# Seven half products instead of a plain second product in 14 of 18 expert slots, with the first expert's slots beside attention and the second's behind it

## The chip, the cores and the metric

The kernel runs on one core of a Trainium2 chip. The metric is the device time of one execution in microseconds. The engines are named as in the profile: PE (TensorE, the matrix engine; PEld is its loading of weights), DVE (VectorE), ACT (ScalarE), POOL (GpSimd) and SP (SyncE, which here only issues DMAs). Each engine works through its own instructions in the order in which the kernel issues them, and semaphores tie the engines together.

## The reference

Windowed attention, followed by a mixture of experts in which every row goes to one expert. All data are float32.

```python
# q, k, v: (8, 8, 576, 64): batch, heads, positions, head width
scores = q @ k.T / 8            # a position sees itself and the 63 before it
attn   = softmax(scores) @ v
x      = attn, rows of 8 heads side by side      # (4608, 512)
logits = x @ w_gate + modality_bias[modality_id] # 8 experts
e      = argmax(logits);  gate = softmax(logits)[e]
out[i] = gate[i] * (relu(x[i] @ w1[e]) @ w2[e])  # w1: 512 x 1024, w2: 1024 x 512
```

The two modalities have biases that favour one expert each, so most rows go to two experts. The kernel calls the one with the larger lead X (or 0) and the other Y (or 1), and picks them on the chip from the biases.

## The kernel before, in words

**Attention.** The 4608 rows are 36 pairs of 64-row blocks, one pair (128 rows) per step `s` of the main loop; two steps are a group `G` (256 rows). Step `s` does the scores of pair `s`, the transposed probabilities of pair `s-1`, the values of `s-2`, the logits of `s-3`; steps 36 to 39 only finish. In odd steps the group `R = (s-5)/2` is routed: `route2` (matmuls on PE that count ranks), `route3` (small DVE operations, queued in the list `routing`, the last of which write the rows' target index and scatter them by POOL's indirect DMA into `xs`, a DRAM buffer ordered by expert). `tick(n)` issues n of these small operations; five or six at a time.

**Slots.** Expert work is done in slots of 256 rows (two tiles `t` of 128). A slot loads its rows from `xs` into the one buffer `xt`, transposes them (`x_part`), takes the first product in four quarters `first(sl, k, i)`, k = 0 to 3, each two pieces i (12 matmuls of 256 columns, in three terms of high and low parts, since every operand is split into two numbers of the type fp32r), a relu on ACT and a low part on DVE, and then the second product. In a plain slot the second product is eight pieces `second(sl, k, t)` of 6 matmuls of 512 columns. In a slot marked `fast` it is seven products of halves (a Winograd form of Strassen's scheme): `left_of` and `right_of` make parts and sums of the four blocks of the hidden rows, `rest_of` two more, `product` takes p1 to p7, each 12 matmuls of 256 columns, and `fast_out` adds them into the output tiles with the gate. The sums of the four blocks of W2 that this needs are made in `combine`.

**Order.** The generator `slot_pieces` yields after each piece, 16 to a plain slot and 15 to a fast one. From step `FIRST = 12` on the main loop calls it at four fixed gaps of a step (`gap`), between attention's parts, and behind attention the last `while` loop runs it to its end. Work of other engines that follows a piece is put into `later` and issued at the next `run_later`. The order on every engine is this issue order. PSUM has eight banks: two for "tp", one each for "sp0", "sp1", "av", "em", "y0" and "y1". `bank(i)` gives the first product's bank: "em" for even quarters, and for odd ones "em" as well while the list `last` is empty, which is so during attention, then "sp0".

**Which slot holds what.** `EARLY` names the groups T after whose scatter a count is taken and a slot is planned (`plan`), and for which of X and Y. The load of such a slot waits only for the scatters up to T (`scatter_after_T`). `LATE` lists slots behind attention: two of X; then the two Y slots that were held back; three of any expert, and a half slot. So there are X, X, X, X, Y, Y, Y, Y, X, X, X, X, X, Y, Y, any, any, any, half; the fast ones are the five X slots from the ninth on (`MIXED = 7`). Rows that these leave would go to a loop with a dynamic trip count at the end (lines 1445 to 1532); it makes no trip here, and the profile has no instruction of it.

**Weights.** Both experts' weights lie in SBUF as high and low parts (`Whi`, `Wlo`), loaded in 32 pieces (`weights`, `split_hi`, `split_lo`) from step 4 on. Behind attention the "any" slots' pieces are swapped in place (`swaps`). The eight `pads` copy rows of padding behind each expert's rows in `xs`; no late slot is loaded before them.

## Time and profile before

| what | value |
|---|---|
| time, three runs | 645.15 us median (641.67 to 645.71) |
| profiled execution, its own time | 640.05 us |
| its span, first to last instruction | 638.3 us |
| PE busy | 611.4 us, 96% |
| DVE busy | 403.5 us, 63% |
| ACT busy | 328.5 us, 51% |
| POOL busy | 154.3 us, 24% |
| matmuls | 6689 |
| granted PE clock | 0.999 of full |

Attention's last scores are at about 332 us, its last logits at some 358 us, and what follows to 638 us is expert slots alone. A row of groups has the line, the engine, the operation, the tiles out<-in, shapes and count, then busy microseconds, mean nanoseconds of one, and the idle time before them with what ended it. A row of a timeline has its start, its length, engine, line, operation and tiles, and in brackets the engine's idle time before it and what ended it. The chain of waits follows the work that ended last back to what released it. Matmuls are pipelined: their listed durations overlap, and distances between starts give the pace.

### The profile page before, as it was taken

To read this page: it belongs to the slowest core of one execution; us is meant where nothing else is said; L and a number is where in the kernel's file an instruction comes from. 1 tells how busy PE (TensorE), PEld (TensorE's weight loads), DVE (VectorE), ACT (ScalarE), POOL (GpSimd) and SP (SyncE) were. 2 spreads that over 40 slices of the span, in tenths; PEclk is the share of its full clock that TensorE was granted. 3 is DMA by queue.
4 is the path that set the end of the run, shared out by engine and by line. 5 is a ranking of instruction groups with operands and counts; after the bars stand their busy time and mean duration, and the time that the engine had idled before them with its cause. 6 is when DMAs were issued, how large, how long until landed. Compare 5 with 4: busy or idle time off the path is not lost. (4 is left out here: it accounts for less than half of the span.)

```text
span 638.3 us, 17909 instructions
## 1 busy us (share of the span) xinstructions
PE 611.4 (96%) x6689; PEld 558.0 (87%) x6689; DVE 403.5 (63%) x1571; ACT 328.5 (51%) x1005; POOL 154.3 (24%) x337
## 2 busy tenths in 40 slices
PE   6898888999999999999999999999999999999996
PEld 3787777898989889899898988999999989989886
DVE  2978977666776676756654255876746755666611
ACT  3888876656665656455644123533433444554411
POOL 5324432042032213320322255111011011101102
PEclk9999999999999999999999999999999999999999
DMA  9989894774876674552323476021105076777300
GB/s 170 184 194 249 233 222 133 180 167 121 184 177 151 140 177 106 142 137 57 111 75 110 123 205 242 20 67 51 50 34 198 16 223 198 211 243 240 109 1 36
DMA packets 142120, 90.72 MB, mean 142 GB/s; under 512 B 118954, under 2 KB 118992, under 8 KB 141904
## 3 DMA queue, kind: packets, MB, share of 16 engines
q1 hardware_dynamic: 133344, 70.07, 44.8%
q0 software_dynamic: 5856, 18.92, 8.0%
q10 hardware_dynamic: 2832, 0.59, 0.6%
q8 instruction: 53, 0.87, 0.6%
q14 instruction: 35, 0.29, 0.2%
HBM read 70.11 MB, written 23.91 MB: 147 GB/s over the span
## 5 line engine op out<-in xcount | busy, mean ns | idle before, releaser
L290 PE MATMUL em<-xh,Whi 128*128 128x256 f32 x400 | 102.8, 291 | 1.2 <-DVE xl L196 1.0
L290 PE MATMUL em<-xh,Wlo 128*128 128x256 f32 x400 | 98.2, 279 | 0.0
L765 ACT ACTIVATE ss<-ss,mn 128x128 f32<-128x128 f32 x240 | 94.0, 397 | 2.6 <-DVE mn L753 2.6
L429 POOL DMA_INDIRECT out_dram<-y,id x36 | 37.5, 1042 | 219.3 <-DVE y L394 74.4
L415 PE MATMUL y<-Whi,hh 128*128 128x512 f32 x208 | 86.6, 416 | 0.0
L415 PE MATMUL y<-Wlo,hh 128*128 128x512 f32 x208 | 81.6, 392 | 2.2 <-DVE e_take L154 2.2
L415 PE MATMUL y<-Whi,hl 128*128 128x512 f32 x208 | 81.5, 392 | 0.0
L290 PEld LDWEIGHTS em<-xh,Whi 128*128 128x128 f32 x400 | 75.3, 188 | 2.2 <-DVE xl L196 1.6
L290 PEld LDWEIGHTS em<-xh,Wlo 128*128 128x128 f32 x400 | 75.4, 188 | 0.5
L774 ACT COPY pT<-tp 128x512 f32<-128x512 f32 x59 | 32.6, 589 | 78.6 <-PE tp L595 74.3
L753 DVE CUSTOM_DVE_ANT_0 ss<-sp,masks 128x128 f32<-128x128 f32 x240 | 53.5, 287 | 18.4 <-PE sp L736 16.2
L301 DVE SCALAR_TENSOR_TENSOR hl<-em,hh 128x512 fp32r<-128x512 f32 x40 | 27.6, 690 | 57.1 <-ACT hh L300 57.1
L290 PE MATMUL em<-xl,Whi 128*128 128x256 f32 x400 | 63.2, 280 | 0.0
L892 POOL DMA_INDIRECT xs_scratch<-xa,idx x36 | 36.2, 1007 | 81.4 <-DVE lm L835 26.2
L290 PEld LDWEIGHTS em<-xl,Whi 128*128 128x128 f32 x400 | 53.7, 188 | 0.0
L791 PEld LDWEIGHTS av<-ve,pT 128*64 128x64 f32 x576 | 36.3, 138 | 16.4 <-issue 8.4
L300 ACT ACTIVATE hh<-em 128x512 fp32r<-128x512 f32 x40 | 23.6, 591 | 48.1 <-PE em L290 44.1
L791 PE MATMUL av<-ve,pT 128*64 128x64 f32 x576 | 41.0, 225 | 7.2 <-DVE ve L666 3.3
L415 PEld LDWEIGHTS y<-Whi,hl 128*128 128x128 f32 x208 | 39.0, 188 | 8.8
L765 ACT ACTIVATION_READ_ACCUMULATOR ss<-ss,mn 128x1 f32 x240 | 46.4, 193 | 0.0
L415 PEld LDWEIGHTS y<-Wlo,hh 128*128 128x128 f32 x208 | 39.2, 189 | 7.6 <-DVE e_take L154 2.5
L415 PEld LDWEIGHTS y<-Whi,hh 128*128 128x128 f32 x208 | 39.1, 188 | 5.6 <-ACT Whi L112 0.3
(341 smaller groups left out, 1535.3 us busy)
## 6 DMA issues: line engine op xcount, KB each, us to landing
xt<-xs_scratch SPq DMA_DIRECT2D x18, 514.0 KB
y<-in_moe_w_dram SPq DMA_DIRECT2D x32, 256.0 KB
vo<-in_v_dram SPq DMA_DIRECT2D x27, 256.0 KB
vo<-in_moe_w_dram SPq DMA_DIRECT2D x27, 256.0 KB
ss<-in_moe_w_dram SPq DMA_DIRECT2D x27, 256.0 KB
pT<-in_moe_w_dram SPq DMA_DIRECT2D x18, 256.0 KB
xs_scratch<-xs_scratch SPq DMA_DIRECT2D x8, 514.0 KB
qk<-in_q_dram SPq DMA_DIRECT2D x16, 256.0 KB
```

What stands on the lines that cost most here:

```text
L290: nc.tensor.matmul(out=hb[:, i * TP:(i + 1) * TP], lhsT=w[buf][:, c0:c0 + P], rhs=x[:, c * TP:(c + 1) * TP], start=(n == 0), stop=(n == le ...
L300: nc.scalar.activation(out=hh, in_=hb, func=AF.Relu),
L301: nc.vector.scalar_tensor_tensor(out=hl, in0=hb, scalar=0.0, in1=hh.bitcast(F32), op0=ALU.max, op1=ALU.subtract)))
L415: nc.tensor.matmul(out=sl["y", t], lhsT=h[:, i * TP + t * P:i * TP + (t + 1) * P], rhs=w[buf][:, c0:c0 + DM], start=(k == 0 and n == 0), s ...
L429: ins = nc.gpsimd.indirect_dma_start(out=out, out_offset=bass.IndirectOffsetOnAxis(ap=sl["id"][:, t:t + 1], axis=0), in_=y, in_offset=None ...
L753: nc.vector.tensor_tensor_reduce(out=ss[a][:, hp, :], in0=sp[a][:, hp * P:(hp + 1) * P], in1=mask, scale=-1.0 / 8.0, scalar=3.0e38, op0=AL ...
L765: nc.scalar.activation(out=ss[a][:, hp, :], in_=ss[a][:, hp, :], func=AF.Exp, bias=mn[:, h:h + 1], scale=-1.0, accum_out=sm[:, h:h + 1])
L774: nc.scalar.copy(out=pT, in_=pp)
L791: nc.tensor.matmul(out=av[c * W64:(c + 1) * W64, 2 * hp + a], lhsT=pT[:, i:i + W64], rhs=(vo if c else ve)[p][:, 2 * hp + a, :], start=Tru ...
L892: ins = nc.gpsimd.indirect_dma_start(out=xs, out_offset=bass.IndirectOffsetOnAxis(ap=idx[:, j:j + 1], axis=0), in_=xg[j], in_offset=None)
```

## The change

All slots beside attention are now X's, at T = 2, 4, ..., 16, and one more X slot follows; then seven slots of Y, two of any expert and the half slot: again 18 full slots and a half. Slots 0 and 1 are plain; the 14 from the third X slot to the last Y slot are fast, five of them wholly beside attention. A piece order of its own is used there (`late7` is false): quarter 1 and quarter 2 follow one another, p7 stands ahead of quarter 3, and the first product's relu for the next slot is queued behind p3. The parts of `right_of` that make sums are a function of their own, `sums_of`, queued later by `after`. Products have only "y0" and "y1" while attention runs.

Only X's weights are loaded beside attention. Their memory is cut into other tiles: `M0` to `M3` hold X, `S0` X's sums of W2, `S1` and `S2` the parts of the fast slots beside attention. X's sums are made in steps 16 to 19, Y's in steps 36 to 39 (`SUMS`). Y's weights come behind attention: the first matrix during slot 7, into `S1` and `S2`; the second during slot 8, over X's first matrix. The padding is ten copies instead of eight: X's and Y's first, which the late X and the Y slots wait for; the others during slots 10 to 12.

```diff
-    EARLY = ((2, (0, 1)), (4, (0, 1)), (6, (0, 1)), (8, (0, 1)), (9, (1, 2)), (10, (1, 2)), (11, (1, 2)),
-             (12, (0, 2)), (13, (0, 2)), (15, (0, 2)))
+    EARLY = tuple((T, (0, 1)) for T in (2, 4, 6, 8, 10, 12, 14, 16))
...
-    LATE = ((0, False), (0, False), (0, True), (1, True), (0, True), (1, True))
-    NPIN = 2
+    LATE = ((0, False),) + ((1, False),) * 7 + ((2, True), (3, True), (2, True))
+    NPIN = 7
...
+    PLAIN = 2
...
-    stock = [wpool.tile([P, 2 * WC], F32, name=f"W{part}1") for part in ("hi", "lo")]
-    Whi = [wpool.tile([P, 2 * WC], F32R, name="Whi0"), None]
-    Wlo = [wpool.tile([P, 2 * WC], F32R, name="Wlo0"), None]
+    stock = [wpool.tile([P, 2 * WC], F32, name="S0")] + [wpool.tile([P, WC], F32, name=f"S{n}") for n in (1, 2)]
+    w_x = [wpool.tile([P, WC], F32R, name=f"M{n}") for n in range(4)]
+    store = {0: w_x}
...
+    def run_after():
+        later.extend(after)
+        after.clear()
...
-        fast = n_slots[0] > MIXED and buf == 0 and whichever is None
+            fast=n_slots[0] > PLAIN and whichever is None, n=n_slots[0] - 1)
...
             if i == 1 and sl["fast"]:
                 later.append(lambda: (left_of if k < 2 else right_of)(sl, k % 2, hb))
+                if k >= 2:
+                    after.append(lambda: sums_of(sl, k % 2, hb))
...
+        def sums_of(sl, k, hb):
+
+            if "s1" not in sl:
+                sl["s1"] = [att.tile([P, ROW], F32R, name=f"xa{i}")[:, 0:512] for i in (0, 4)]
             a12, a22 = halves_of(hb)
             a11, a21 = halves_of(sl["r", k])
             nc.vector.scalar_tensor_tensor(out=a21, in0=a22, scalar=0.0, in1=a21, op0=ALU.max, op1=ALU.add)
             nc.vector.tensor_tensor(out=a11, in0=a21, in1=a11, op=ALU.subtract)
+            s4 = sl["t"][:, k * TP:(k + 1) * TP].rearrange("p (c t) -> p c t", t=P)
+            nc.vector.scalar_tensor_tensor(out=s4, in0=a12, scalar=0.0, in1=a11, op0=ALU.max, op1=ALU.subtract)
             parts(a21, sl["s1"], k)
...
+            order = ("p1", "p7", "p2", "p4", "p5", "p6", "p3")
+            i = order.index(nm)
+            if last:
+                home, n = ("y0", "y1", "sp1", "av")[i % 4], i // 4
+            else:
+                home, n = ("y0", "y0", "y1", "y1")[i % 4], i % 2
...
             if sl["fast"]:
+                for k in (1, 2):
+                    for i in range(2):
+                        first(sl, k, i)
+                        yield
+                fast_step(sl, "p1")
+                run_after()
                 yield
+                late7 = bool(last)
+                if not late7:
+                    fast_step(sl, "p7")
+                    yield
+                first(sl, 3, 0)
                 yield
                 nxt = fetch()
                 first(sl, 3, 1)
                 yield
+                if late7:
+                    fast_step(sl, "p7")
+                    run_after()
+                    yield
                 fast_step(sl, "p2")
+                run_after()
+                if late7:
+                    later.append(lambda: rest_of(sl, "s2"))
                 yield
                 fast_step(sl, "p4")
+                later.append(lambda: rest_of(sl, "s4" if late7 else "s2"))
                 yield
                 x_part(nxt, 0)
                 run_later()
                 x_part(nxt, 1)
+                if last:
+                    run_later()
                 fast_step(sl, "p5")
+                if not late7:
+                    later.append(lambda: rest_of(sl, "s4"))
                 yield
                 fast_step(sl, "p6")
                 yield
                 first(nxt, 0, 0)
                 yield
                 first(nxt, 0, 1)
+                if not late7:
+                    after.append(later.pop())
                 yield
                 fast_step(sl, "p3")
+                run_after()
                 yield
...
-            pieces.extend((x, c) for x in range(2) for c in PIECE_ORDER)
+            pieces.extend((0, c) for c in PIECE_ORDER)
...
+    SUMS = {FIRST + 4 + j: (0, j) for j in range(4)}
+    SUMS.update({NPR + j: (1, j) for j in range(4)})
...
-        n_tick = 6 if s < FIRST else 5
+        n_tick = 6 if s < FIRST or j else 5
...
+    last.append(True)
+    tick(ready_p - issued[0], table=True)
+    pad_rows(pads.pop(0))
...
+    at_ = begin_of[slot_y - 2] + 1
+    for c in (0, 2, 4, 6, 1, 3, 5, 7):
+        task(at_, whole_piece(1, c, 1), load(at_, c, lambda: evs[1]))
+    at_ = begin_of[slot_y - 1] + 7
+    pairs_y = [[load(at_, 8 + j + 4 * i, lambda: evs[1]) for i in range(2)] for j in range(4)]
+    for n in range(6):
+        if n < 4:
+            task(at_, y_quarters(n), *pairs_y[n])
+        if 0 < n < 5:
+            task(at_, lambda x, y: combine(x, y, False), *pairs_y[n - 1])
+        if n > 1:
+            task(at_, y_fourth(n - 2), *pairs_y[n - 2])
```

The weights of the "any" slots follow in the same way as tasks, one piece of work to a step of the `while` loop: the first one's spread over slots 10 to 14 into `M2`, `M3` and `S0`, the others' during the plain slots 16 and 17.

## The prediction

> **What bounds the kernel now.** I read the page first, for which engine is full and when.

> ```profile
> span 638.3 us, 17909 instructions
> PE 611.4 (96%) x6689; PEld 558.0 (87%) x6689; DVE 403.5 (63%) x1571; ACT 328.5 (51%) x1005; POOL 154.3 (24%) x337
> PE   6898888999999999999999999999999999999996
> DVE  2978977666776676756654255876746755666611
> PEclk9999999999999999999999999999999999999999
> ```

> PE is full from the eighth slice (about 112 us) to the last but one, at full granted clock; the loads before that and the end are not touched by the change. So the time is the sum of PE's work plus every wait that is put into PE's queue. Next I read the chain of waits in order of time, which after attention is PE alone, and gives each slot's length (rows: start, length, what).

> ```profile
> 461.06 2.81 PE em L290 x24
> ...
> 476.56 1.44 PE sp L374 x12
> ...
> 482.99 2.81 PE em L290 x24
> ...
> 527.96 2.81 PE em L290 x24
> 530.78 1.38 PE y L415 x6
> ...
> 550.96 2.81 PE em L290 x24
> ```

> From one first product's second quarter to the next slot's, a slot by seven products takes 482.99 - 461.06 = 21.93 us, a plain one 550.96 - 527.96 = 23.00 us: 1.07 us apart. The third view is the busy time of stretches: attention without any weights work, seven-product slots, and plain slots with weight pieces. The last row is the DVE time of line 119 alone, the weight pieces, in the third stretch.

> ```profile
> 240.00:280.00 40.00, 40.00 (x530) 35.99 (x532) 25.20 (x122) 21.71 (x80) 11.24 (x22) 1.00 0.49 121
> 440.00:480.00 40.00, 40.00 (x346) 40.00 (x345) 23.15 (x53) 15.97 (x35) 4.91 (x12) 1.00 0.11 41
> 520.00:560.00 40.00, 40.00 (x268) 36.31 (x267) 25.40 (x42) 19.73 (x37) 5.86 (x12) 1.00 0.67 210
> ...
> 520.00:560.00 40.00, 16.33 (x27) 1.00 0.67 210
> ```

> The columns after the stretch are PE, PEld, DVE, ACT, POOL. DVE needs 23.15 x 21.93/40 = 12.7 us for a seven-product slot and (25.40 - 16.33) x 23.00/40 = 5.2 us for a plain one: 7.5 us more. In attention a slot lasts some 41 us (four steps), and DVE there has 40 - 25.2 = 14.8 us free in 40. So DVE would go to about 32.5 of 40: it is not the bound by its sum, but it and ACT answer PE more slowly, and the question is who waits for an answer.

> **The change, part by part.**

> *The arithmetic.* 14 slots instead of 5 lose one piece each: 9 x 1.07 = 9.6 us off PE, wherever they lie, as PE is full throughout. The trace's rows under it are 1.44 us for 12 matmuls of 256 columns and 1.38 us for 6 of 512, 120 and 230 ns each. [...]

> *Where the slots lie.* From step 13 on a step runs four pieces, so piece p after the first four is in step 13 + (p-1) div 4, at gap (p-1) mod 4. Slots 0 and 1 stay plain (pieces 1 to 32), slots 2 to 5 are by seven products in full attention (33 to 92), slot 6 in steps 36 to 39 (93 to 107), slots 7 to 15 behind attention. Those behind attention behave as the five of before, whose 21.93 us hold no stall. Inside attention two things differ, both unknown to this trace and priced from its nearest rows.

> *One PSUM bank for the first product.* While `last` is empty `bank(0)` and `bank(1)` are both "em", with one buffer. A plain slot puts two second-product pieces between two quarters of the first product. The new order issues quarter 2 straight behind quarter 1 (waiting for the relu of `left_of`), and quarter 1 of the next slot behind p3, with that relu queued only after p3; and p2 straight behind quarter 3 needs that quarter's relu and its low part. The rows show when these answers come today. Each case is a piece of PE, and ACT's relu and DVE's low part for the quarter before it:

> ```profile
> 231.34 0.47 PE L415 MATMUL y<-Whi,hh 128*128 128x512 f32 x1
> 231.81 0.59 ACT L300 ACTIVATE hh<-em 128x512 fp32r<-128x512 f32 x1
> 232.43 0.69 DVE L301 SCALAR_TENSOR_TENSOR hl<-em,hh 128x512 fp32r<-128x512 f32 x1 [0.30 <-ACT hh L300]
> ...
> 265.41 0.48 PE L415 MATMUL y<-Whi,hh 128*128 128x512 f32 x1
> 266.40 0.58 ACT L300 ACTIVATE hh<-em 128x512 fp32r<-128x512 f32 x1
> 267.02 0.69 DVE L301 SCALAR_TENSOR_TENSOR hl<-em,hh 128x512 fp32r<-128x512 f32 x1 [1.58 <-ACT hh L300]
> ...
> 295.49 0.58 ACT L300 ACTIVATE hh<-em 128x512 fp32r<-128x512 f32 x1
> 295.54 0.48 PE L415 MATMUL y<-Whi,hh 128*128 128x512 f32 x1
> ...
> 296.24 0.68 DVE L301 SCALAR_TENSOR_TENSOR hl<-em,hh 128x512 fp32r<-128x512 f32 x1
> ...
> 354.56 0.48 PE L415 MATMUL y<-Whi,hh 128*128 128x512 f32 x1
> ...
> 354.67 0.60 ACT L300 ACTIVATE hh<-em 128x512 fp32r<-128x512 f32 x1 [0.76 <-PE em L290]
> ```

> The relu ends behind the start of the next piece by 1.06 us after gap 0 (ACT does xaT's copy first), 1.57 after gap 2 (exps and a copy first), 0.53 after gap 1, and 0.71 near the end of attention; after gap 3 the long stretch of attention covers it. Today that costs nothing, since the next piece is in another bank. With the change these are PE waits. By the gaps above, quarter 2 behind quarter 1: slot 2 at gap 1 (0.53), slot 3 at gap 0 (1.06), slot 5 at gap 2 (1.57), slot 4 covered. Quarter 1 behind p3: after slot 2 at gap 2 (1.57), slot 3 at gap 1 (0.53), slot 4 at gap 0 (1.06), slot 5 covered. Together 6.3 us. p2 needs the low part at its ninth matmul, 8 x 0.12 = 0.96 us in: slot 3 at gap 2, 267.71 - 265.41 - 0.96 = 1.34; slot 4 at gap 1, 296.92 - 295.54 - 0.96 = 0.42; slot 5 at gap 0, 233.12 - 231.34 - 0.96 = 0.82; 2.6 us. Slot 6 adds two of 0.71, 1.4 us. The bounds of these eleven: nothing if ACT came earlier; and, with more in ACT's and DVE's queues,

> ```profile
> L308 ACT CAST ve<-xa 128x256 fp32r<-128x256 f32 x20 | 8.1, 406 | 3.8 <-DVE xa L348 2.8 <-DVE masks L154 0.7
> ```

> two more such parts (0.41 us each) ahead at each of the nine places in full attention, 7.3 us more. I take four of these eighteen, 1.6 us, as a seven-product slot spreads its parts over four steps and few can stand right ahead of a relu.

> *Rows of group 16 for slot 7.* EARLY now ends at T = 16, whose rows are scattered in step 37; slot 7's load is fetched at piece 100 (gap 3 of step 37), and its transposes are piece 103 (gap 2 of step 38). Only two steps of little attention lie there. The rows show the chain of such a load, and the routing matmul of step 37:

> ```profile
> 106.57 0.17 DVE L904 CAST idx<-dst 128x2 int32<-128x2 f32 x1
> 109.08 0.97 POOL L892 DMA_INDIRECT xs_scratch<-xa,idx  x1 [0.28 <-POOL xa L891]
> 112.57 0.39 SPq L206 DMA_DIRECT2D xt<-xs_scratch  x1
> 116.41 0.19 POOL L274 COPY gate<-xt 128x2 f32<-128x2 f32 x1 [3.89 <-DMA xt<-xs_scratch]
> ...
> 354.51 0.19 PE L863 MATMUL tp<-oh,ones 128*128 128x16 bf16 x2
> 355.97 0.15 DVE L873 TENSOR_TENSOR tgt<-tp,ebase 128x16 f32<-128x16 f32 x1
> 356.46 0.22 DVE L886 RECIPROCAL xa<-se 128x1 f32<-128x1 f32 x2
> 357.47 0.64 PE L816 MATMUL tp<-wg,xaT 128*64 128x8 f32 x16
> ...
> L394 DVE SCALAR_TENSOR_TENSOR y<-y,gate,y 128x512 f32<-128x512 f32 x10 | 7.5, 747 | 0.4
> ```

> From the index to rows in SBUF: 116.41 - 106.57 = 9.8 us. From routing matmul to index: 0.7 us of small operations (355.97 to 356.68) behind one 0.75 us output of p7 (line 394), and the index itself, now within the step, as its ticks go from 5 to 6: 1.7 us. PE has in that time the quarter 3 pair (2.8), the logits of step 38 (0.6), p2 and p4 (2.9): 6.3 us. So PE waits 9.8 + 1.7 - 6.3 = 5.2 us. Bounds: 3 us if nothing lies ahead of the index and the load is quicker, 8 if POOL's new subtractions stand before the scatter. Slot 6 (T = 14) has a step of full attention more, and none is counted. SP waits behind this scatter with the Y sums of step 39 queued behind the load; they go to slot 9 and are early by far.

> *Work with cover.* Y's 16 pieces leave attention, and X's sums enter in steps 16 to 19, on engines that are not the bound: nothing. Y's pieces go to slots 7 and 8: 12.7 + 8 x 16.33/27 = 17.5 us of DVE in 21.9: covered; without cover it would be the 4.8 us. The X pad, its wait on SP and slot 8's load have ten pieces, 14 us, after attention: nothing taken, 4 us as the upper bound. The ten pads instead of eight, and table operations moved to slots 9 to 13: DVE has over 4 us free in each slot. The last slots (two plain, a half) are as before.

> *The sum.* -9.6 + 6.3 + 2.6 + 1.4 + 1.6 + 5.2 = +7.5 us. The profiled execution took 640.05 us (span 638.3 and 1.8 around it), under the median of the runs shown, 645.15 (641.67 to 645.71). It becomes 647.6, and on the median's level 652.7.

> What speaks most against this change beside the waits themselves is what a wait may bring. The longest that the waits view has for PE is

> ```profile
> PE y L415 <- DVE e_take L154: 2.2, 1, 2.2
> ```

> and the granted clock is 9 in every slice. [...]

> **The rivals.**

> *Forecast*: waits outweigh the gain, 652.7; its own range 648 to 660. Chance 0.50.

> *The waits stay covered* (not slower): ACT gets the relu early enough, because the exps move away from it once PE is held, and only the load costs: 645.15 - 9.6 + 5.2 = 640.8; with the load early as well, 635.5. For: DVE has 14.8 us in 40 free in attention, ACT 18.3. Against: each relu in the rows above ends after the next piece began. It decides where the relu ends before PE reaches the next em piece. Chance 0.12, two thirds of it at 635.5.

> *Waits as large as the gain*: the lower row (0.53) at the nine places in attention, 4.8, with 1.4 and a load wait of 3: -0.4, 645. Chance 0.20.

> *DVE becomes the bound in attention.* Its queue is in order, and it stands idle at a head that waits for ACT:

> ```profile
> DVE hl L301 <- ACT hh L300: 82.4, 45, 4.9
> ```

> 1.8 us each time. A seven-product slot has some eight heads of that kind where a plain one has four. Four more at 1.8 put 32.5 of 40 to 39.7, and any burst then is PE's: 2.5 us more a slot in slots 2 to 5, 10 us, 663. Against: waits shrink when a queue is behind. Chance 0.12.

> *Half clock behind the 5.2 us wait*: as long a stretch at half rate adds 2.6 us, 655.6. No row bears it out. Chance 0.04. *A group's count does not fill its slot*, a slot runs on dummy rows, and another is paid for at 23.0 us: 676. All early slots of before were full, as the fallback loop left no row. Chance 0.02.

> **How the numbers follow.** The predicted time is the forecast's, 652.7. The range 640 to 664 takes in the covered case down to its load wait, and the DVE case; it leaves out 0.08 below and some 0.07 above. About 1% (6.5 us) is what a measurement tells from no change. Faster: the fully covered case, 0.08. Same: its rest 0.04, the equal case 0.20, and the forecast's part below 651.6, 0.14: 0.38. Slower: 0.54.

> **What would show it.** Right: in steps 21 to 34 PE matmuls of line 290 idle on ACT's relu, a fraction to 1.6 us each, and p2 on DVE's low part; one PE wait of 4 to 6 us for the load of xt near the end of attention; slots behind it at 21.9 us. Wrong: PE's idle in attention no larger than before, transposes of slot 7 not waiting, or DVE above 37 of 40 in attention.

## The result: 714 us instead of 644, and the profile after

The changed kernel took **714.37 us** (711.16 to 715.27), the kernel before **644.06 us** (641.67 to 645.71) beside it: a ratio of 1.109, interval 1.103 to 1.114. The forecast was 652.7, with a range from 640 to 664. The direction was right and the size was far off: +70 us where +7.5 was worked out.

The page of the changed kernel, where the profiled execution took 715.27 us (span 713.5 and 1.8 around it):

```profile
span 713.5 us, 18839 instructions
PE 640.4 (90%) x7010; PEld 596.4 (84%) x7011; DVE 474.9 (67%) x1755; ACT 363.0 (51%) x1109; POOL 177.3 (25%) x365
PE   6898799999988898998879868798699999999996
DVE  2879867767657576685567553868867777657662
PEclk9999999999998999999999979799899999999999
```

PE was full from the eighth slice on; now it has holes from slice 12 (196 us) to slice 29 (517 us), and only behind them is it full again. The clock strip shows that something else is gone: two slices at 7 and two at 8.

The waits of PE, longest sums first (who waits, for what: us, times, longest):

```profile
PE y L398 <- DVE y L418: 8.5, 6, 2.7
PE y L398 <- ACT y L416: 6.5, 4, 1.9
PE em L292 <- ACT S L340: 6.3, 7, 1.2
PE y L398 <- ACT xa L312: 5.7, 1, 5.7
PE sp L398 <- ACT hh L352: 5.2, 2, 2.7
PE em L267 <- DMA xt<-xs_scratch: 4.8, 3, 4.2
...
PE em L292 <- DVE xl L196: 3.1, 2, 2.0
...
PE sp L398 <- DVE hl L353: 2.1, 2, 1.8
```

Line 292 is the first product, 398 the seven products, 267 the transposition of a slot's rows. The third and the sixth row are terms of the forecast: 6.3 us where 6.3 was forecast, and 4.8, of which one wait of 4.2, where 5.2 was. The first two, 15.0 us, are not in it at all, nor are the fourth, the fifth and the one for `xl`, 14.0 us, of which 13 lie behind attention (1.0 us of the one for `xl` stands ahead of slot 1, as before the change).

Two stretches in full attention (PE, PEld, DVE, ACT, POOL, then the granted clock, DMA share and GB/s) answer to the row at 240 us of the prediction:

```profile
200.00:240.00 40.00, 34.22 (x363) 31.91 (x362) 24.94 (x111) 21.04 (x74) 6.09 (x14) 0.87 0.32 81
240.00:280.00 40.00, 35.02 (x455) 32.65 (x455) 26.54 (x115) 22.12 (x76) 5.49 (x14) 0.96 0.37 93
```

PE lacks 5 to 6 us in 40, and the clock is at 0.87 and 0.96. DVE is busy for 25 to 27 of 40 us, hardly more than before: nobody is full, everybody waits.

The length of each slot, worked out from the timeline as the time from the first transposition of one slot's rows to that of the next (us):

| slot | before | after | after again (693) | e1 tiles | e3 tail | e7 all four | e8 plain, tail | e18 |
|---|---|---|---|---|---|---|---|---|
| 2 | 43.2 | 48.9 | 44.3 | 41.8 | 44.3 | 41.8 | 42.9 | 42.9 |
| 3 | 43.9 | 52.3 | 50.4 | 47.5 | 50.4 | 44.8 | 42.9 | 42.9 |
| 4 | 43.1 | 51.6 | 47.8 | 45.2 | 47.8 | 49.4 | 42.9 | 42.9 |
| 5 | 40.9 | 51.7 | 48.7 | 43.4 | 48.7 | 41.2 | 40.6 | 40.6 |
| 6 | 29.9 | 43.3 | 41.5 | 40.1 | 41.6 | 42.0 | 29.9 | 29.9 |
| 7 | 23.1 | 38.8 | 39.1 | 36.5 | 33.5 | 26.3 | 25.2 | 23.8 |
| 8 | 21.9 | 22.6 | 24.0 | 22.0 | 22.4 | 22.3 | 22.0 | 23.9 |
| 9 | 22.3 | 26.3 | 24.9 | 24.8 | 27.3 | 27.3 | 27.2 | 22.7 |
| 10 | 21.9 | 29.4 | 29.3 | 29.3 | 21.9 | 22.0 | 21.9 | 23.5 |
| 11 to 15, each | 21.9 to 23.1 | 21.9 | 21.9 | 21.9 | 21.9 | 21.9 | 21.9 | 21.9 |

"Before" and "after again" are the runs e15 and e16 below, on one chip. Slots 11 to 15 are what the forecast promised. Nearly everything is lost in slots 2 to 7, 9 and 10. Not in the table is slot 0, which got shorter: 38.1 us in e16 against 42.2 in e15. There PE waits 2.2 us in the kernel before (the row of 2.2 us on `e_take` that the prediction shows), in e15 with a window of half clock in it, and 0.2 in after.

### The profile page after: what moved, and what is told of

Same layout as the page of the kernel before. It is cut to its first block, busy times and chain, and to the rows that moved or that the text cites. A ratio compares the mean times of both kernels' runs of the same rounds, so it can differ in the third digit from the quotient of the medians.

```text
span 713.5 us, 18839 instructions
## 1 busy us (share of the span) xinstructions
PE 640.4 (90%) x7010; PEld 596.4 (84%) x7011; DVE 474.9 (67%) x1755; ACT 363.0 (51%) x1109; POOL 177.3 (25%) x365
## 4 chain that ended last, share of the span: by engine, by line
PE 74%; DVE 6%; issue 5%; ACT 4%; DMA 2%; SPq 0%; POOL 0%; POOLq 0%; ACTq 0%
PE em L292 19%; PE y L398 12%; PE tp L631 8%; PE sp L292 8%; PE y L439 6%; PE sp L771 5%; PE av L826 5%; PE sp L398 3%; PE tp L851 2%; PE av L398 1%; DMA xt<-xs_scratch 1%; DMA ss<-in_moe_w_dram 1%; ACT y L416 1%; PE y L493 1%; ACT ss L800 1%
## 5 line engine op out<-in xcount | busy, mean ns | idle before, releaser
L292 PE MATMUL em<-xh,M 128*128 128x256 f32 x560 | 84.5, 294 | 8.1 <-ACT S L340 6.3
L809 ACT COPY pT<-tp 128x512 f32<-128x512 f32 x59 | 32.5, 590 | 113.3 <-PE tp L631 113.2
L292 PEld LDWEIGHTS em<-xh,M 128*128 128x128 f32 x560 | 73.1, 195 | 10.1 <-ACT S L340 7.8
L771 PE MATMUL sp<-kT,qT 64*64 64x128 f32 x1152 | 50.1, 290 | 5.3 <-issue 2.3
L418 DVE SCALAR_TENSOR_TENSOR y<-y,gate,y 128x256 f32<-128x256 f32 (+1 forms) x85 | 45.8, 566 | 13.1 <-PE y L398 11.3
L771 PEld LDWEIGHTS sp<-kT,qT 64*64 64x64 f32 x1152 | 35.9, 139 | 11.2 <-issue 7.0
L292 PE MATMUL em<-xl,M 128*128 128x256 f32 x280 | 44.7, 282 | 0.0
L292 PEld LDWEIGHTS em<-xl,M 128*128 128x128 f32 x280 | 38.4, 191 | 0.0
L292 PE MATMUL em<-xh,S 128*128 128x256 f32 x256 | 36.4, 285 | 2.0 <-DVE xl L196 2.0
L292 PEld LDWEIGHTS em<-xh,S 128*128 128x128 f32 x256 | 33.5, 194 | 2.4 <-DVE xl L196 2.2
L292 PE MATMUL sp<-xh,S 128*128 128x256 f32 x256 | 35.2, 280 | 0.0
L826 PE MATMUL av<-vo,pT 128*64 128x64 f32 x480 | 35.2, 228 | 0.0
```

The lines of the kernel that those rows point to most:

```text
L292: nc.tensor.matmul(out=hb[:, i * TP:(i + 1) * TP], lhsT=wap(buf, w, c0, P), rhs=x[:, c * TP:(c + 1) * TP], start=(n == 0), stop=(n == len( ...
L418: nc.vector.scalar_tensor_tensor(out=y, in0=in_, scalar=g, in1=y, op0=ALU.mult, op1=ALU.add)
L771: nc.tensor.matmul(out=sp[a][c * W64:(c + 1) * W64, hp * P:(hp + 1) * P], lhsT=qT[rows, g // GBLK, hp, g % GBLK + c], rhs=blocks(hp, g, g ...
L809: nc.scalar.copy(out=pT, in_=pp)
L826: nc.tensor.matmul(out=av[c * W64:(c + 1) * W64, 2 * hp + a], lhsT=pT[:, i:i + W64], rhs=(vo if c else ve)[p][:, 2 * hp + a, :], start=Tru ...
```

## The experiments

### First: how much of the 70 us belongs to the change

The kernel unaltered, on two further chips, and the kernel before once more:

> The changed kernel itself, unaltered, on the chip of the next three runs. In the trace of after, TensorE lost about 1.2 us in every second step of attention at the score products, waiting for nothing that the profile shows; the run without the queue block and the burst of tables, whose attention code is the same, had none of these gaps and 17 us less in slots 1 to 6. If these 17 us belong to the kernel: 711-715 again. If they belong to the placement of that run (the code's fetch or the phase of the clock's windows): 695-703, and the three runs before are to be read against that.

> The kernel before, unaltered, for a trace from the chip of the next three runs. If that chip shows gaps at the score products that wait for nothing (7.0 us of the idle time ahead of their weight loads in the first run of the changed kernel, 6.3 us in the run with the split four pieces later), this trace tells whether the kernel before has them too. Theory 'they belong to the chip': then it has them, and its time is above 645. Theory 'they belong to the changed code': it has none in either case, 639-643.

> The changed kernel a third time. With gaps at the score products 709-715, without them 691-699.

Measured: 695.88 us (690.95 to 699.23) beside 640.29, ratio 1.086 (1.080 to 1.092); then 694.12 us (692.57 to 698.98) beside 640.42, ratio 1.087 (1.083 to 1.091); the kernel before, traced there, 641.22. So some 55 us are the change's in all three, and some 18 came on top in the first. The score products show where most of these came. First the run of 714 us, then that of 694 (busy and mean ns; then idle ahead of them and what ended it):

```profile
L771 PE MATMUL sp<-kT,qT 64*64 64x128 f32 x1152 | 50.1, 290 | 5.3 <-issue 2.3 <-DVE qT L754 0.8 <-ACT qT L754 0.7
L771 PEld LDWEIGHTS sp<-kT,qT 64*64 64x64 f32 x1152 | 35.9, 139 | 11.2 <-issue 7.0 <-ACT qT L737 1.1 <-DVE qT L754 1.0
```

```profile
L771 PE MATMUL sp<-kT,qT 64*64 64x128 f32 x1152 | 41.1, 280 | 2.5 <-DVE qT L754 0.9 <-ACT qT L754 0.8 <-DVE qT L737 0.5
L771 PEld LDWEIGHTS sp<-kT,qT 64*64 64x64 f32 x1152 | 31.8, 135 | 4.1 <-DVE qT L754 1.0 <-POOL hl L1109 0.9 <-ACT qT L737 0.8
```

In the first run PE stood before score products with nothing to wait for that the profile shows ("issue"): matmuls and the idle time ahead of them are 50.1 + 5.3 against 41.1 + 2.5, 11.8 us more. That run also had 16 windows of half clock where the later one had 11. Three kernels below (e12, e13, e14) show the same gaps on one further chip, where the kernel before took 642.7 us; one of the three, run again elsewhere, lost 12 us of its time and the gaps with them. So the gaps depend on the chip. Whether the kernel before has them too is open: e15 was to show it, and ran on a chip where the changed code has none either; by its times, 2 to 4 us longer on the two chips with gaps, it loses less there than the changed code. What makes them is open. The experiments are read against 695 us. One chip alone gave times from 691 to 699 for the changed kernel; e1, e2, e3, e4, e6, e9, e10 and e12 below are one run each, and differences of a few us between them and others say little unless the slots show the same.

### e1: the tile that products share

In attention the products fill y0, y0, y1, y1, so that p7 writes beside p1 in one tile, and p4 beside p2.

```diff
-                home, n = ("y0", "y0", "y1", "y1")[i % 4], i % 2
+                home, n = ("y0", "y1")[i % 2], i // 2 % 2
```

> The changed kernel, but during attention the seven products alternate between the two output tiles (y0, y1, y0, y1) instead of filling the halves of one tile one after the other (y0, y0, y1, y1). Theory 'shared tile': TensorE's waits on the output of the product just before (groups 'PE y <- ACT y' 6.5 us and 'PE y <- DVE y' 8.5 us) fall to under 3 us in all; the half-clock stretches that begin beside them (205, 226, 277, 328, 373 us; 20.5 us long) go too and give back about 10 us; the time falls from 714 to 688-697. Theory 'waits only, clock unimportant': 700-704. Rival 'the engines' queues are late anyway': the wait passes to the relu, the split parts or the next product, and the time stays above 709.

Measured: 674.75 us, some 20 us less than 695; slots 2 to 6 take 217.9 us, where e16 took 232.6. The waits of e1:

```profile
PE em L292 <- ACT S L340: 6.4, 7, 1.2
PE y L398 <- ACT xa L312: 5.7, 1, 5.7
PE em L267 <- DMA xt<-xs_scratch: 5.4, 2, 5.0
PE sp L398 <- ACT hh L352: 5.1, 2, 2.9
```

The two rows on line 398 that headed the list are gone, and the half clock in slots 2 to 5 with them. The loss was not what the products take but that p7, p4 and p6 each wrote into the tile that ACT or DVE was still reading for the product before. In after, p7 starts behind an output of ACT that ends at 204.34:

```profile
203.07 1.27 ACT L416 ACTIVATE y<-y,gate 128x512 f32<-128x512 f32 x2
...
204.40 1.86 PE L398 MATMUL y<-S,S 128*128 128x256 f32 x11 [1.84 <-ACT y L416]
```

It starts 0.06 us behind that end, after 1.84 us of waiting. Alternating between the two tiles is worth some 20 us here, without another buffer.

### e2 and e3: attention and the stretch behind it

e2 keeps slots 2 to 6 plain:

```diff
-    PLAIN = 2
+    PLAIN = 7
```

> The changed kernel, but the fast form starts with the eighth slot instead of the third: the five slots beside attention take the second product whole, as before; loads, pads, tables and order of slots are those of the changed kernel. Slots 2 to 6 were 46.8 us longer than before. Theory 'two separate losses' (attention, and the stretch behind it): slots 2 to 6 go back to 40-44 us each (30 us the last), slots 7, 9 and 10 keep their 27 us over the kernel before: 664-671. Rival 'the stretch behind attention is late only because the fast slots leave ScalarE and VectorE behind': 640-650. My prediction's terms alone (em, p2, slot 6's waits, queue lag: 11.9 us, less 5 x 1.07 of gain) would give 707.

e3 mends two places behind attention: the split of a piece of weights waits for four more pieces behind its load, and the table operations run ahead.

```diff
-        if n_task < len(tasks) and tasks[n_task][0] <= t:
+        if n_task < len(tasks) and tasks[n_task][0] <= t and all(
+                put_at[i] + 4 <= waited for i in tasks[n_task][2]):
...
-        if t >= begin_of[slot_y] + 8:
-            tick(1)
+        tick(2 if t >= begin_of[slot_y] or -5 <= t - begin_of[slot_y - 1] < 8 else 1)
```

> The changed kernel, but behind attention (a) a piece of weights is split only four pieces after its load is issued, so that ScalarE's queue does not stand on a DMA, and (b) the table operations are issued two at a time from slot 8 on, so that no burst of 40 stands ahead of the first load of an any-expert weight. Theory 'queue blocked by the DMA, burst of tables': the waits of 2.5 and 2.8 us in slot 7 and of 5.7 us in slot 10 go, and with them the half-clock stretches at 448 (10.2 us) and 509 (6.8 us), which cost about 8.5 us: 692-698. Without the clock's part: 702-704. Rival 'these waits only stand in for others' (order of SyncE's issues, the load of slot 7): above 709.

Measured: e2 647.29 us, e3 682.07 us. e2 has the time of its rival, but half of the rival's reason: slots 2 to 6 are back at 42.9 (40.6 and 29.9 the last two), and of the loss behind them only slot 7's went down (26.8 us, from 39); slots 9 and 10 keep theirs (24.9 and 29.6). So most of slot 7's loss comes from the fast slots ahead of it, while slots 9 and 10 have a cause of their own.

e3 finds both. In after, DVE's timeline ahead of slot 10 (start, us, instruction; some forty lines of one element to sixteen are left out):

```profile
502.67 0.15 DVE L154 TENSOR_TENSOR masks<-sel 1x8 f32<-1x8 f32 x1
...
510.68 0.14 DVE L142 TENSOR_SCALAR bias_sel<-bias_sel 1x1 int32<-1x1 f32 x1
510.77 0.75 DVE L418 SCALAR_TENSOR_TENSOR y<-y,gate,y 128x512 f32<-128x512 f32 x1
511.44 0.41 DVE L362 SCALAR_TENSOR_TENSOR xa<-sp,xa 128x256 f32<-128x256 f32 x1
```

For 8.1 us DVE works through table operations that the first load of an any-expert weight forces out at one spot; the sums (line 362) for p5 stand behind them, and PE waits 5.7 us. Spread out, slot 10 takes 21.9 us. And ACT's timeline in slot 7 of after:

```profile
435.28 0.41 ACT L312 CAST xaT<-y 128x256 fp32r<-128x256 f32 x1 [0.42 <-issue]
443.48 0.62 ACT L114 CAST S<-vo 128x512 fp32r<-128x512 f32 x1 [7.80 <-DMA vo<-in_moe_w_dram]
...
445.07 0.59 ACT L352 ACTIVATE hh<-em 128x512 fp32r<-128x512 f32 x1
```

ACT's queue is in order: the split of Y's first piece stands 7.80 us on its DMA, and quarter 2's relu (line 352), whose product was done by 438, stands behind it. PE waits for that relu and the next, 5.2 us. The two mendings give 695 - 682 = 13 us, where 16 to 22 were expected. Most of it is slot 10 (21.9 us, from 29.3) and slot 7 (33.5, from 39.1).

### e4: what a wait of PE does to the clock

Most waits of after are 1 to 3 us long, yet the clock was halved ten times. e4 measures that alone, in the kernel before, whose tail has no wait.

```diff
+    def chain(hops):
+        tp = ps_t.tile([P, 512], F32, name="tp")
+        turn(tp[:, 0:P], ident)
+        src = tp[W64:P, 0:P]
+        for i in range(hops):
+            (nc.scalar.copy if i % 2 else nc.vector.tensor_copy)(out=z[i % 2], in_=src)
+            src = z[i % 2]
+        turn(tp[:, P:P + W64], src, W64)
```

> The kernel before, with one artificial wait of TensorE in each of nine slots behind attention, where it otherwise never waits: a transposition, then 1, 2, 3, 4, 5, 6, 8 copies in a chain over VectorE and ScalarE, then a transposition of the last copy; in the last two slots two chains of 2, and four chains of 1, in consecutive pieces. Estimated waits, at about 0.35 us a copy: 0.5 to 3.0 us, in the last two slots 2 x 0.85 and 4 x 0.5. Theory 'a wait of over 3 us in one piece halves the clock': at most the chain of 8 shows 0.50. Theory 'idle time of some 2 us within a few us is enough': the chains of 5, 6 and 8 show it, perhaps the two chains of 2 as well. Each stretch is 3.4 us or a multiple and costs half its length; the waits add about 15 us, so 660 us with no stretch, some 5-7 us more with three or four of them.

Measured: 676.79 us. The waits, which also hold what stood in the two queues ahead of the copies, came out at 2.9, 1.5, 1.4, 1.8, 2.0, 2.4, 2.9, then 1.2 and 0.7, then 0.8, 0.4, 0.4 and 1.6 us (PE's idle time ahead of the second transposition). The clock was halved behind the first (2.9), the fifth (2.0), the seventh (2.9) and the last group, not behind the sixth (2.4). The stretches of half clock begin on a grid of 3.413 us (410.28, then 29, 15 and 18 steps later), so the windows of that grid show why:

```profile
406.87:410.28 3.41, 1.44 (x11) 1.38 (x12) 1.64 (x8) 0.40 (x1) 0.69 (x4) 1.00 0.20 77
410.28:413.69 3.41, 3.41 (x18) 3.41 (x17) 1.55 (x4) 1.12 (x3) 0.00 (x0) 0.50 0.00 0
...
505.85:509.27 3.42, 1.68 (x13) 1.61 (x14) 0.94 (x4) 0.59 (x2) 0.20 (x2) 1.00 0.01 5
509.27:512.68 3.41, 3.41 (x18) 3.41 (x17) 1.93 (x5) 1.50 (x3) 0.00 (x0) 0.50 0.00 0
529.75:533.16 3.41, 1.87 (x11) 1.29 (x9) 1.81 (x4) 1.47 (x4) 0.14 (x1) 1.00 0.66 230
533.16:536.57 3.41, 2.55 (x15) 2.22 (x16) 2.12 (x4) 2.18 (x5) 0.00 (x0) 1.00 0.32 89
557.05:560.47 3.42, 0.57 (x4) 0.17 (x2) 2.00 (x6) 1.37 (x5) 0.00 (x0) 1.00 0.27 77
560.47:563.88 3.41, 3.33 (x9) 2.64 (x10) 1.89 (x3) 1.69 (x4) 0.00 (x0) 0.50 0.27 74
...
618.49:621.90 3.41, 1.78 (x12) 1.35 (x11) 2.03 (x4) 1.62 (x3) 0.33 (x3) 1.00 0.57 208
621.90:625.32 3.42, 3.42 (x10) 2.65 (x9) 0.27 (x2) 0.62 (x1) 0.00 (x0) 0.50 0.49 158
```

The first number behind the comma is PE's busy time, the number behind the five engines the clock. A window with PE busy for 1.44, 1.68, 0.57 or 1.78 of 3.41 us is followed by one at 0.50; one with 1.87 is not, although its wait was longer (2.4 us) than that of 1.68 (2.0 us): it lay across a border of the grid. One such window costs about 1.5 us: slot 12 took 26.1 us, of them 21.9 its own, 2.0 the wait and 0.7 the chain's own matmuls (slot 10: 24.0 with a wait of 1.4). The first theory of the expectation falls, as 2.0 us are enough; the second is nearer, but what the half clock goes with is neither one wait nor their sum, it is the busy share of a window that neither theory knew (the last section counts it over more traces).

### e6, e7: the waits that I had forecast, and all four mendings

e6 adds to e1 the relu right behind its quarter and another order of pieces, so that a product stands between two quarters that use `em`.

```diff
+                if k < 2:
+                    later.append(lambda: relu_of(sl, k, hb))
...
-  p5, p6, quarter 0, p3, quarter 1, quarter 2, p1
+  p5, quarter 0, p6, quarter 1, p3, quarter 2, p1
```

> The kernel with alternating output tiles, and beside it: during attention the relu of a quarter is issued right behind the quarter, apart from the rest of that step, and the order of pieces is quarter 0, p6, quarter 1, p3, quarter 2, so that a product stands between two quarters that share the bank em. Theory 'em waits' (my prediction's 6.3 us): the waits 'PE em <- ACT S' (1.2-1.35 us each) fall to nearly none, and the time from 674.8 to 667-671. Rival 'ScalarE's and VectorE's queues are the limit': the parts of a quarter are now later for p1, TensorE waits there instead, 673-680.

(The lines on the order are in words, not code.) Measured: 674.39 us, against e1's 674.75; slots 2 to 6 take 216.8 and 217.9. The 6.4 us of em waits are gone (0.4 us is left), and the time is the same within what two single runs can tell. The waits of e6 that e1 had smaller or not at all:

```profile
PE tp L647 <- DVE xa L850: 3.7, 2, 3.4
...
PE tp L647 <- DVE lg L872: 3.2, 4, 1.8
```

They were 0.6 and 2.0 us in e1: attention's own output and logits, now behind the fast slot's sums in DVE's queue. The rival of the expectation is the one that came.

e7 is e6 with e3's two mendings.

> Alternating output tiles, relu and order of pieces as in the run before this one, and behind attention the split of weights four pieces behind its load and the table operations spread. If the causes add up: the 667-671 of the run before, less 7.4 us in slot 10 and some 4 us in slot 7: 655-661, still slower than the kernel before (641), by what is left in slots 3 to 7 and 9. If they stand in for one another: above 664.

Measured: 661.20 us (660.39 to 661.63) beside 640.29, ratio 1.033 (1.031 to 1.034). The totals add up: 695 less 20 (e1) less 13 (e3) is 662. The slots do not: slot 7 gives 12.8 us where e1 and e3 alone give 2.5 and 5.5, and slots 2 to 6 take 1 to 2 us more than in e1 and e6, with 13.7 us of half clock in them against 1.6 and 4.9.

### e8, e9, e10, e12: what is left is the fast form beside attention

e8 is e3 with plain slots in attention (`PLAIN = 7`), so e7 less e8 is the fast form's own cost there.

> Plain slots beside attention (fast from the eighth slot on), with the split behind its load and the tables spread. The run with plain slots alone took 647.3 us, of them 5.7 us of a wait in slot 10 and about 2 us of half clock beside it. Theory 'the burst is a cost by itself': slot 10 at 22 us, 637-641, which is the kernel before or up to 0.6% faster: four more slots at 21.9 instead of 23.0 us give 4.3 us, of which slots 7 to 9 still take some 5. Rival 'the burst passes to slot 9': 644-647.

Measured: 639.13 us (637.54 to 644.33), ratio 0.999 (0.997 to 1.001). So the fast form in five slots beside attention still costs 22 us where it was to gain 5. 200 us of attention, e7 first, then e8:

```profile
165.00:365.00 200.00, 190.39 (x2564) 179.66 (x2562) 145.98 (x631) 118.08 (x405) 56.70 (x107) 0.98 0.38 105
```

```profile
165.00:365.00 200.00, 199.51 (x2486) 179.47 (x2483) 120.42 (x583) 103.16 (x363) 63.33 (x121) 1.00 0.41 115
```

DVE has 25.6 us more to do, ACT 14.9, and neither is near 200; PE lacks 9.6 us in e7 and 0.5 in e8. Over slots 2 to 6, 20 us longer in e7, PE idles 12.3 us against 0.5, and 13.7 us run at half clock against none. Three runs take this apart. e9 and e10 start from e7, e12 from e8.

```diff
 e9    in attention the low part's tile is the high part's, and its subtraction is left out
 e10   (nc.scalar.copy if last else nc.gpsimd.tensor_copy)(out=two[0], in_=src)
 e12   ten more nc.vector.tensor_tensor of 128 x 256 a slot, two or three behind each quarter's low part
```

> The kernel with all four mendings (661.2 us, 22 us over the same kernel with plain slots beside attention, 639.1), without the subtractions that make the low parts of the sums in the slots beside attention; the products use the high part in their place, so that TensorE's work is the same. It leaves out ten VectorE instructions of 0.42 us in each of five slots, 21 us of VectorE's time, and gives up the low part of these sums. Theory 'VectorE's queue is late' (it is busy 28.9 of 40 us against 24.0 with plain slots, in order, and attention's own waits on it grew): the time falls by more than half of the 22 us, to 642-650. Rival 'ScalarE's queue' or 'the clock alone': 656-661.

> The kernel with all four mendings, but in the slots beside attention the ten copies that make the high parts (ScalarE, 0.41 us each, 4.1 us a slot) are GpSimd's, which is busy only 10.5 of 40 us. Theory 'ScalarE's queue is late': 648-656. Rival 'VectorE's queue': 658-664, or more where GpSimd's copies (about 0.75 us each, by its subtractions of the same size) are late for the products.

> Plain slots beside attention with the tail's two mendings (639.1 us), and in each of the five slots beside attention ten more VectorE subtractions of 128 x 256 (0.42 us each, as in the fast form), behind the low parts of the quarters; nothing waits for their result. Leaving ten such out of the fast slots gave 11 us in slots 2 to 6. Theory 'a longer VectorE queue alone delays attention': 646-652. Rival 'it costs only where TensorE waits for the sums themselves': 638-641.

Measured: e9 653.16 us, between its two expectations; slots 2 to 6 take 208.2 us together, where e7 took 219.2, e6 with the same code in attention 216.8, and e8 199.2. So the ten subtractions a slot, without which the products lack the low part of their sums, stand for 9 to 11 of these 18 to 20 us; the whole run gained 8. e10 666.78 us: giving ACT 15 us less to do in these slots gained nothing, but the copies came later, not sooner. DVE's subtractions waited 12.4 us for POOL's copies there and 6.1 us for ACT's in e7, although a copy takes 0.41 us on either. So e10 does not show what a less loaded ACT would be worth. e12 655.20 us, on the chip with the gaps (e13 and e14 there: 648.5 and 650.6). Its attention beside that of e14, first e12, then e14:

```profile
165.00:365.00 200.00, 195.11 (x2440) 173.54 (x2439) 130.93 (x597) 103.98 (x374) 56.73 (x110) 1.00 0.40 110
```

```profile
165.00:365.00 200.00, 196.79 (x2444) 174.81 (x2443) 115.05 (x565) 104.56 (x373) 55.73 (x111) 1.00 0.40 110
```

15.9 us more of DVE's time take 1.7 us from PE, and slots 2 to 6 take 208.5 us against 207.2. So DVE's time as such is cheap, as far as this chip shows it: its gaps make the same slots 8 us longer than e8's, and could cover part of the price. The same instructions are dear where they stand in a bunch at one spot of the program and in a chain: relu, high part, low part, product. That it is the bunch, and not the chain, was not separated.

### e11, e13, e14, e17, e18: the change's tail alone

With plain slots in attention, most of what is left of the loss is slot 9, where the split of Y's second weights keeps DVE busy ahead of its low part of x: 2.6 us, and 1.5 us of half clock. e11 issues no table operation there; e13 also begins that split four pieces later, e14 two.

```diff
-    at_ = begin_of[slot_y - 1] + 7
+    at_ = begin_of[slot_y - 1] + 11
...
+        tick(0 if -5 <= t - begin_of[slot_y] < 9 else 2)
```

> Plain slots beside attention, split behind its load, as in the run of 639.1 us; but no table operation is issued in the thirteen pieces in which the second pinned expert's second weights are split (slots 8 and 9), and two a piece before and after. There VectorE was busy without a gap from 404 to 416 us and the x of slot 9 came 2.5 us late, with 1.5 us of half clock behind it. Theory 'the tables are what is too much': slot 9 at 22-24 us, 634-637, faster than the kernel before (640.3) by 0.5 to 1%. Rival 'the split of weights alone fills VectorE': slot 9 at 26-27 us, 638-640.

> As the run of 638.7 us, but the split of the second pinned expert's second weights begins four pieces later, behind the x of slot 9, no table operation is issued from five pieces ahead of slot 9 to nine behind, and the first any-expert weights are loaded eight pieces later. Theory 'the split stands ahead of the x of slot 9 in VectorE's queue': the waits of 1.1 and 2.0 us for xl go, slots 8 and 9 take 22-23 us: 634.5-636.5. Rival 'the work only moves': p1 or p2 of slot 9 wait for the factors instead, 638-640.

> The same with the split two pieces later instead of four, and no table operation from seven pieces ahead of slot 9 to five behind. Theory 'the split stands ahead of the x of slot 9': some two of the six tasks ahead of the x are left, so half of the gain: 636-638. Rival as in the run before: 638-640.

> The kernel that took 638.7 us (0.997 of the kernel before), beside the next one on one chip. Without gaps 637-640; with them 649-653.

> The split four pieces later again, which was timed only on a chip with gaps (648.5 us). By its slots 7 to 10 (23.9, 23.8, 22.7, 23.5 us, against 24.1, 23.8, 24.9, 22.4 of the kernel of the run before this one) it is 1.3 us faster than that: ratio to the kernel before 0.993-0.997 without gaps. Rival 'it makes the gaps by itself': 647-651 while the run before it takes 637-640.

Measured: e11 638.72 us, ratio 0.997 (0.9957 to 0.9985), slot 9 at 24.9 us; the rival had the time. e13 648.48 (ratio 1.009, 1.007 to 1.011) and e14 650.64 (1.010, 1.007 to 1.013) on the chip with gaps. On one without, e17, which is e11's kernel, took 638.64 (0.996, 0.994 to 0.998) and e18, which is e13's, **636.67 us** (636.26 to 637.65) beside 640.42, **ratio 0.995 (0.993 to 0.996)**. The page of e18:

```profile
span 635.0 us, 18326 instructions
PE 610.3 (96%) x6830; PEld 565.8 (89%) x6831; DVE 433.1 (68%) x1645; ACT 340.0 (54%) x1049; POOL 174.9 (28%) x365
PE   6998889999999999999999998999999999999996
```

PE is full again from slice 8 on, with 1 us less of busy time than before and one slice at 8. This is the fastest version, half a per cent under the kernel before; e11 and e17 are 0.3 to 0.4% under it. It keeps of the change the order of slots and the fast form behind attention, and gives up the fast form beside it. But the fast form is not where its gain lies. Beside e15, traced on the same chip, three of the four further fast slots give 3.3 us over slots 11 to 17, and slots 7 to 10, with the fourth, lose 4.7; slots 2 to 6, plain in both, are 2.0 us shorter, and slot 0 is 4.1 us shorter, as the wait of 2.2 us there and its half clock are gone. That the halved weight loading in attention removed this wait is likely and was not tested.

## Why the prediction was wrong, step by step

- **The arithmetic, -9.6**: right. Slots 11 to 15 take 21.9 us, and with separate tiles slot 2 takes 41.8 against 42.9 plain, 1.1 us.
- **Waits at `em`, +6.3**: the waits came where they were forecast, 0.4 to 1.2 us each where 0.53 to 1.57 was put down. The six in slots 2 to 5 hold 5.7 us for 6.3, the one in slot 6 0.69 for 0.71; that the seven make 6.3 again is chance. As a cost the term was wrong: e6 took the waits away and gained nothing that one run can show. A wait that I took from a row stood for another wait behind it.
- **p2 on the low part, +2.6 and +1.4**: in after these two groups (p2 on hh and hl in attention) hold 1.4 us where 2.6 and one of slot 6's 0.7 were put down; the step is right and its size less than half.
- **Queue lag, +1.6**: this is the step that failed in attention. I counted the parts that might stand ahead of a relu, and left out that the outputs of the seven products stand in the same two queues, with the next product writing into the same tile: 15.0 us of waits, some 20 us by e1. The line with the homes is in the diff; I priced the banks of the first product and not those of the second.
- **Slot 7's load, +5.2**: right as a wait, 4.2 us in after, 3.7 to 5.0 in e1, e3, e5, e6 and e16 and 3.0 in e7. What came behind it was priced at nothing in the sum: three windows of half clock in after, e3 and e16; in after PE was busy for 8.5 us of them, so that, by an estimate from the granted 0.50, about 4 us more were lost.
- **Work with cover, nothing**: this is the step that failed behind attention. I compared sums ("DVE has over 4 us free in each slot"; 17.5 us of split in 21.9), and the loss was in the order: 8.1 us of table operations at one spot, and a split that holds ACT's queue on a DMA for 7.8 us; e3 mends these two for 13 us. Slots 7, 9 and 10 lost 16.0 + 2.6 + 7.4 us in the run of 694 us (39.1, 24.9 and 29.3 against 23.1, 22.3 and 21.9), where 5.2 was forecast. The bounds of 4.8 and 4 us did not hold either. Slot 7's part is not all the order's: e3 takes 5.5 us off it, plain slots ahead (e2) 12.2.
- **The rival "half clock", 0.04**: the mechanism was real, and its condition wrong. I tied it to one wait of over 5 us. In after it struck in ten stretches, 16 windows, most behind waits of 1.7 to 2.7 us. The load's wait of 4.2 us brought it too, as the rival said, but for 10.2 us and not for 5.2 (652.7 and 2.6 also make 655.3 and not 655.6). At half a window each, 1.7 us (an estimate from the granted 0.50; e4 showed about 1.5), the 16 are at most 27 us, less where PE waited anyway. That it takes so long a wait was shown by no view of before, whose longest is 2.2 us; e4 halves the clock behind 2.0 us.
- **The rival "DVE becomes the bound"**: fell. DVE was to reach 32.5 of 40 us and was at 25 to 27 in after; e12's 15.9 us more of DVE alone made slots 2 to 6 1.3 us longer, on its chip. What the fast form adds to DVE was forecast well: 8.0 us a slot in slots 2 to 6 (e16 against e8), where 7.5 was worked out.
- **"the loads before that and the end are not touched by the change"**: slot 0 is 4.1 us shorter in all traces of the changed code without gaps than in e15, as a wait of 2.2 us and its half clock are gone. The forecast has no such gain; it made the miss smaller by luck.

By the runs, the 55 us are: 20 from the shared tile, 13 from the two queues behind attention, 22 from the rest of the fast form beside attention (9 to 11 of them with the low-part subtractions), and nearly -1 for what is left, e8 beside the kernel before. In that last part slots 7 to 10 lose 7.1 us in e8's trace against e15's, which the 3.1 us of slots 11 to 17 do not pay for; slots 0 and 1 give 4.0 and slots 2 to 6 2.1. The 18 us of the first run are beyond that. What makes the 22 us cost so much, the bunch of DVE's instructions or the chain that they lengthen, stays open.

## What to carry to other kernels

An engine with free time hid work here only if its queue reached that work in time (ACT, 51% busy in after, let PE wait 5.2 us behind a split that stood 7.80 us on its DMA): read for each in-order queue what stands ahead of the instruction that PE will wait for, not how full the engine is, and be wary of any code that issues a batch of small operations, or waits for a DMA, at one spot. Where a product here wrote one half of a tile while another engine still read the other half, the two ran one after the other, although they share no column (in after p7 waited 1.84 us for the output and began 0.06 us behind its end); go to the other tile first. And a wait in the list is a price only if nothing stands behind it: e6 removed 6 us of waits for no gain.

## What the hardware showed that was not expected

**Gaps of PE that wait for nothing** cost the changed code and its variants 12 to 18 us in the first run and on one further chip, and nothing on four others. The kernel before has no such gap in its two traces, of which e15's comes from a chip without gaps; beside the runs that have them it took 642.7 and 644 us, elsewhere 640 to 641. They were seen at the score products above all; their cause was not found.
